# X and C in one set of loads, and XA loaded whole and copied into place by GpSimd

## The chip, the cores and the metric

The kernel runs on one core of a Trainium2 chip. The metric is the device time of one execution in microseconds; the time given for a kernel is the median of its runs. A profile shows one execution, with the time of every instruction on the five engines (TensorE, VectorE, ScalarE, GpSimd, SyncE) and of the DMA traffic.

## The reference

The kernel computes three layers, one after the other, over 3072 tokens (4 batches of 768) of 256 features:

```
# 1. a state-space layer, per batch and head (8 heads of 32), in chunks of 32 tokens
L = exp(cum_i - cum_j), causal;  M = (C B^T) * L
y[chunk] = M @ x + (C @ state) * exp(cum)
state = exp(sum log a) * state + sum_j decay_j * B_j x_j^T
# 2. a mixture of 8 experts, one per token
e = argmax(x @ w_gate);  out = gate * relu(x @ w1[e]) @ w2[e]
# 3. a dense layer
out = relu(x @ w_in)^2 @ w_out
```

The change is in the first layer. There `x` is needed in two layouts: by chunk and position for the state update (called Xt here), and by position for `M @ x` (called XA). `C` is needed in two as well (Cb for `C B^T`, CT for `C @ state`).

## The kernel before

The function `attention` does layer 1 and the gating of layer 2. The work is cut into 6 phases (two batches by 256 tokens each) of 4 tiles (128 tokens by 256 features), 24 tiles in all. One loop, `for i in range(-2, 24)` (L672), issues everything in an order written out by hand; each engine works its own instructions strictly in that order and waits on semaphores for the others. In step `i` of the loop:

- `st_S(i + 2)` (L416): TensorE multiplies B by Cb into `sc` (L425), VectorE multiplies by the decays Qm into M (L428). It has work for two of the four tiles of a phase.
- `st_D(i + 2)` (L431): TensorE multiplies the decayed B (Bt) by Xt into `dS` (L444); `st_R(i + 2)` (L451): VectorE runs the state forward with it (L461). Both have work in even steps only.
- `st_Y(i)` (L463): TensorE adds up `M @ XA` (L473) and `CT @ state` (L480); VectorE scales the sum into `row` (L485).
- `prep(ph)` (L387), on GpSimd, makes Qm (L401) and Bt (L395, from the loaded B) of phase `i // 4 + 2`, in step 4n+2: two Qm, two Bt, two Qm, two Bt.
- the gating of finished tiles: transposes, `logits`, `gateA`, `gateB` (which ends in a store of the rows to the DRAM tensor `xs`, L572, on SyncE's queue), `spotA` (VectorE and ScalarE, and one GpSimd multiply into `hi`, L594) and `spotB` (TensorE on `hi`, L602). `row` has three buffers, so the row of phase 3 waits for the store of phase 0.

In this text S(n), D(n), R(n), Y(n) are the work of these functions for tile n; a phase ph has tiles 4ph to 4ph+3.

All loads of this stage are issued by SyncE, in program order, and each tile has two or three buffers. A phase needs: B (`load_b`, one load of 512 KB), CT (`load_t`, two loads of 128 KB), XC (`load_c`, L288: for each of four column blocks `c`, the partitions c, c+4, c+8, ...; Xt and Cb stand side by side in one row, 4 KB each), and XA (`load_x`, L293). XA is block-diagonal: block `c` of the columns is filled in partitions 32c to 32c+31 and is zero elsewhere. The zeros are written once before the loop, and `load_x` brings only the filled part, as four loads of 128 KB (32 partitions of 4 KB).

The order of the loads in the loop, for phases after the second: in step 4n+3 `load_b`, the C half of XC (four loads of 128 KB, `load_c(nx, XS)`, L687), later in the same step XA of the phase before that one (four loads of 128 KB, L751), then CT; in the step after, the Xt half of XC (four loads of 128 KB, L701). Phase 2 has both halves of XC together, in step 0, as four loads of 256 KB. A load waits on SyncE until the last reader of its buffer is done: an XA load for Y of the phase two before it.

The host arranges XA in DRAM as `[phase, 128, 1024]`, partition 32c + j holding block c's rows, so that the four loads of a phase read one contiguous 512 KB.

Of the kernel before, what the change touches and what calls it, by code (L numbers as in the profile page):

```python
# [9 lines left out]
F32 = mybir.dt.float32  # L10
# [232 lines left out]
def attention(tc, k, ctx):  # L243

    nc = tc.nc
    v, s, g, pe, sp = nc.vector, nc.scalar, nc.gpsimd, nc.tensor, nc.sync
# [5 lines left out]
    big = body.enter_context(tc.tile_pool(name="abig", bufs=1))  # L252
# [20 lines left out]
    XA = [(big if p else stp).tile([128, 4, 1024], F32, tag=f"XA_{p}", name=f"XA_{p}") for p in range(2)]  # L273
# [2 lines left out]
    Xr = [x.rearrange("p c (b f) -> p c b f", b=2) for x in XA]  # L276
    BB = [bigs[p // 2].tile([128, 2, 2, 256], F32, name=f"BB_{p}") for p in range(3)]
    CT = [bigs[p // 2].tile([128, 2, 2, 256], F32, name=f"CT_{p}") for p in range(3)]
    Bt = [big.tile([128, 2, 2, 4, 4, NS], F32, name=f"Bt_{p}") for p in range(2)]
    dS = [ps_1.tile([128, 4, 128], F32, name=f"dS_{p}") for p in range(2)]  # L280
    small = k.psk.tile([128, 512], F32, name="small")

    def load_b(ph):
        sp.dma_start(out=BB[ph % 3], in_=k.bb[ph])

    XT, XS = slice(0, 1), slice(1, 2)

    def load_c(ph, at=slice(0, 2), cs=(0, 1, 2, 3)):  # L288
        for c in cs:
            sp.dma_start(out=XC[ph % 2][c:128:4, c].rearrange("p (h f) -> p h f", h=2)[:, at],  # L290
                         in_=k.xc[at, ph, c:128:4].rearrange("h p f -> p h f"))

    def load_x(ph, cs=(0, 1, 2, 3)):  # L293
        for c in cs:
            at = slice(32 * c, 32 * c + 32)
            sp.dma_start(out=XA[ph % 2][at, c], in_=k.xa[ph, at])

    def load_t(ph):
        for h in range(2):
            sp.dma_start(out=CT[ph % 3][64 * h:64 * h + 64, h], in_=k.ct[ph, 64 * h:64 * h + 64])  # L300

# [18 lines left out]
    def zero_t(f, p):  # L320
        for h in range(2):
            o = CT[p][64 * h:64 * h + 64, 1 - h].rearrange("p a f -> p (a f)")
            f(o, zt[64 * h:64 * h + 64])
# [18 lines left out]
    s.activation(la, aa, ACTF.Ln)  # L342
    blank_x(v.tensor_copy, 0, 1)
    load_x(0, (2, 3, 0, 1))
    zero_t(v.tensor_copy, 0)

# [116 lines left out]
    def st_Y(i):  # L463
        ph, r = divmod(i, 4)
        p = ph % 2
        t2, b2 = divmod(r, 2)
        b, t = tile_tokens(i)
        M = Ms[ph, b2]
        y = ps_y.tile([128, 2, 128], F32, tag="y", name="y")
        for hq in range(2):  # L470
            for c in range(4):
                c8 = t2 * 4 + c
                pe.matmul(y[32 * c:32 * c + 32, hq], M[:, hq, c8, :],  # L473
                          Xr[p][:, :, b2, c8 * 64 + hq * 32:c8 * 64 + hq * 32 + 32],
                          start=(hq == 0), stop=False, skip_group_check=True)
        st = states[b, t]
        for hq in range(2):
            for c in range(4):
                s0 = t2 * 128 + c * 32
                pe.matmul(y[32 * c:32 * c + 32, hq], CT[ph % 3][:, hq, b2, s0:s0 + 32], st[:, c],  # L480
                          start=False, stop=True, skip_group_check=True)
        if r == 0:
            rows[ph] = rowp.tile([128, 4, ROW], F32, tag="row", name="row")
        row = rows[ph][:, r]
        v.tensor_tensor(row[:, 0:DM].rearrange("p (h d) -> p h d", d=D), y.rearrange("p q (h d) -> p (q h) d", d=D),  # L485
                        Pd[:, b, t].unsqueeze(2).to_broadcast([128, 8, D]), ALU.mult)
# [30 lines left out]
    def logits2(ph):  # L517
        pe.transpose(small[:, 0:128], gts[ph], ident)
# [57 lines left out]
    def spotA(i, n, late=False):  # L576
        at = k.slots[:, i:i + n]
        lh = pl2.tile([128, 4], I32, tag="lh", name="lh")[:, 0:n]
        lf = pl2.tile([128, 4], F32, tag="lf", name="lf")
        v.tensor_scalar(lh, at, 7, None, ALU.logical_shift_right)  # L580
        v.scalar_tensor_tensor(lf[:, 0:n], lh, -128.0, at, ALU.mult, ALU.add)

        lo = pl2.tile([128, 4, 128], F32R, tag="lo", name="lo")
        hi = pl2.tile([128, 4, NE * NBL], F32R, tag="hi", name="hi")
        some = lambda c, m: cst[:, c:c + m].unsqueeze(1).to_broadcast([128, n, m])
        every = lambda x, m: x.unsqueeze(2).to_broadcast([128, n, m])
        if late:
            v.tensor_tensor(lo[:, 0:n], some(C_LO, 128), every(lf[:, 0:n], 128), ALU.is_equal)
        else:
            for r in range(n):  # L590
                s.activation(lo[:, r], cst[:, C_LO:C_LO + 128], ACTF.Abs, bias=lf[:, r:r + 1], scale=-1.0)
            s.activation(lo[:, 0:n], lo[:, 0:n].bitcast(F32), ACTF.Relu, bias=1.0, scale=-1.0)
        v.tensor_tensor(hi[:, 0:n], some(C_HI, NE * NBL), every(lh, NE * NBL), ALU.is_equal)
        (v if i == 20 else g).tensor_tensor(hi[:, 0:n], hi[:, 0:n].bitcast(F32), every(cst[:, C_ROW + i:C_ROW + i + n], NE * NBL),  # L594
                                         ALU.mult)
        spots[i] = lo, hi
# [37 lines left out]
    def stage(f, i):  # L634
        if 0 <= i < 24:
            f(i)
# [35 lines left out]
    for i in range(-2, 24):  # L672
        if i == 2:
            st_Y(2)
            st_TT(0)
            st_Y(3)
            zero_t(acopy, 2)
            load_t(2)
        if i == -2:
            st_R(0, (0, 1, 2, 3))  # L680
        stage(st_S, i + 2)
        if i >= 0 and i % 4 == 2 and i // 4 + 2 < NPH:
            prep(i // 4 + 2)
        nx = (i + 1) // 4 + 2
        if i % 4 == 3 and 2 < nx < NPH:
            load_b(nx)
            load_c(nx, XS)  # L687
        if i >= 0:
            stage(st_D, i + 2)
        if i % 2 == 0 and 2 < i < 22 and i not in (16, 20):  # L690
            st_TT(i - 2)
        if i in (8, 12):
            spotA(i - 8, 4)
        if i == 18:
            order()
        if i == 6:
            v.tensor_copy(Ub, cst[:, C_U:C_U + 128])
        if 0 <= i < 22:
            st_R(i + 2, (0, 1, 2, 3))
        if i >= 0 and i % 4 == 0 and i // 4 + 2 < NPH:  # L700
            load_c(i // 4 + 2, XT if i else slice(0, 2))  # L701
        if i == 0:
            sp.dma_start(out=cst[:, C_U:C_END], in_=k.consts[:, C_U:C_END])
        if i == 14:
            sp.dma_start(out=k.mc[0:T, :].rearrange("(p q) r -> p (q r)", p=128), in_=blank)
            sp.dma_start(out=k.xs[0:1, :], in_=pad[0:1])
        if i == 17:
            logits2(3)
            gateA(3, 12, 4)
            spotC(8)  # L710
        if i >= 0 and i not in (2, 3):
            st_Y(i)
        if i == 14:
            gateB(2, 8, 4)
            spotA(8, 4)
        if i in (16, 20):
            st_TT(i - 2)
        if i == 16:
            spotB(8, 4)
        if i == 21:  # L720
            logits(4)
        if i in (21, 23):
            st_T(i - 1)
        if i == 23:
            k.ring.low(0, v, 0, 2)
            st_L(20)
            st_L(21)
        if i in (9, 13):
            spotB(i - 9, 4)
        if i in (5, 9, 13, 21):  # L730
            logits2(i // 4 - 1)
            if i in (9, 13):
                spotC(i - 9)
            gateA(i // 4 - 1, i - 5, 4)
        if i == 17:
            gateB(3, 12, 4)
            spotA(12, 4)
        if i == 18:
            spotB(12, 4)
            spotC(12)  # L740
            pick(k.first, 0, 1, 0, 2)
        if 4 <= i <= 16 and i % 4 == 0:
            logits(i // 4 - 1)
        if i == 22:
            st_T(21)
            gateB(4, 16, 4)
            k.ring.high(0)
            k.ring.load(2)
            k.ring.load(3)
        if i >= 3 and i % 4 == 3 and i // 4 + 2 < NPH:  # L750
            load_x(i // 4 + 2)  # L751
        if i % 4 == 3 and 2 < nx < NPH:
            load_t(nx)
        if i in (7, 11):
            gateB(i // 4 - 1, i - 7, 4)
        if i == 18:
            k.moe = Moe(k, tc, k.c2, m0)
            k.ring.aim(0)
            k.moe.load_rows((0, 0))
        if i == 19:  # L760
            k.ring.stage(stp, "XA_0")
            for n in range(2):
                k.ring.load(n)
            early.close()
            k.ring.grow(k.ringpool(), 5)
# [813 lines left out]
```

## Time and profile before

| what | before |
|---|---|
| median of 3 runs (lowest to highest) | 511.66 us (511.46 to 514.49) |
| the profiled execution's own time | 510.4 us |
| its span on the core | 508.4 us |
| TensorE, VectorE, ScalarE, GpSimd busy | 491.3, 372.4, 309.4, 99.4 us |
| DMA traffic | 51.22 MB, mean 101 GB/s |
| granted TensorE clock | 0.998 of full speed |

The span runs from the first to the last instruction. An engine is busy while it executes; TensorE's instructions overlap in its pipeline and their ends are modelled. Layer 1 takes about the first 78 us; the other two layers are long rows of matmuls behind it. A row of a timeline gives the start in us, the time in us, the engine, the line of the kernel, the operation, output and inputs, and how many instructions are merged; in square brackets stands how long the engine had idled before, and which event the profile takes to have ended that. SPq is SyncE's queue of DMA issues: its time is that of the issuing, the data land some microseconds later.

### The profile page before, as it was taken

How to read it: one execution, taken by the hardware profiler on the slowest of the kernel's cores; microseconds unless marked ns; L12 is line 12 of the kernel's file. 1: busy time of each engine (PE TensorE's matmuls, PEld its weight loads, DVE VectorE, ACT ScalarE, POOL GpSimd, SP SyncE). 2: the span in 40 equal slices, each digit the busy share in tenths (PEclk: the TensorE clock that was granted, in tenths of full speed). 3: DMA queues.
4: the chain of work that ended last, by engine and by line, in shares of the span. 5: the costliest groups of instructions: out<-in, count | busy, mean ns of one | idle time of the engine just before them, and what ended most of it. 6: DMA issues, size and time to landing. Idle time of an engine off the chain costs nothing.

```text
span 508.4 us, 11650 instructions
## 1 busy us (share of the span) xinstructions
PE 491.3 (97%) x4537; PEld 459.1 (90%) x4537; DVE 372.4 (73%) x844; ACT 309.4 (61%) x636; POOL 99.4 (20%) x131
## 2 busy tenths in 40 slices
PE   7899798999999999999999999999999999999995
PEld 3677678899999999999999999899999999999995
DVE  8787688669898899994666767534888888676521
ACT  8332335376656666755986889776555555455684
POOL 6953210543331130000000000101500300031031
PEclk9999999999999999999999999999999999999999
DMA  8886866767676656530001100000100000010010
GB/s 258 271 254 219 276 196 209 227 163 191 188 222 169 176 193 191 183 84 2 2 1 43 43 0 1 12 10 12 74 2 0 23 23 1 1 43 1 1 43 24
DMA packets 20476, 51.22 MB, mean 101 GB/s; under 512 B 6561, under 2 KB 6690, under 8 KB 20418
## 3 DMA queue, kind: packets, MB, share of 16 engines
q1 hardware_dynamic: 17442, 43.04, 27.2%
q0 software_dynamic: 2832, 7.01, 5.1%
q8 instruction: 37, 0.61, 0.5%
q10 hardware_dynamic: 144, 0.40, 0.2%
q14 instruction: 21, 0.17, 0.1%
HBM read 44.06 MB, written 6.37 MB: 99 GB/s over the span
## 4 chain that ended last, share of the span: by engine, by line
PE 85%; issue 4%; ACT 3%; DVE 3%; DMA 2%; POOL 1%; SPq 1%; ACTq 0%; another core or an unknown queue 0%; POOLq 0%; DVEq 0%
PE u L1261 24%; PE o L953 14%; PE h L937 14%; PE h L1081 11%; PE h L1169 9%; PE u L1169 2%; DMA XC<-in_xc_dram 2%; PE dS L444 2%; PE y L473 2%; PE sc L425 2%; PE y L480 1%; PE tpm L918 1%; ACT XC L312 1%; PE tp L502 1%; DVE st L461 1%
## 5 line engine op out<-in xcount | busy, mean ns | idle before, releaser
L1261 PE MATMUL u<-wol,ga 128*128 128x256 f32 x384 | 108.0, 281 | 0.0
L1261 PE MATMUL u<-woh,ga 128*128 128x256 f32 x384 | 107.7, 281 | 0.0
L1261 PE MATMUL u<-woh,gb 128*128 128x256 f32 x384 | 107.7, 280 | 0.0
L1275 POOL DMA_INDIRECT out_dram<-ob,idx x24 | 26.6, 1109 | 278.9 <-ACT ob L1274 274.3
L1088 DVE TENSOR_TENSOR gb<-q,ga 128x256 fp32r<-128x256 f32 (+1 forms) x64 | 35.7, 558 | 57.5 <-ACT ga L1087 57.4
L1261 PEld LDWEIGHTS u<-woh,ga 128*128 128x128 f32 x384 | 72.3, 188 | 1.4
L1261 PEld LDWEIGHTS u<-wol,ga 128*128 128x128 f32 x384 | 72.3, 188 | 1.3
L1261 PEld LDWEIGHTS u<-woh,gb 128*128 128x128 f32 x384 | 72.5, 189 | 0.1
L940 ACT ACTIVATE hh<-h 128x256 fp32r<-128x256 f32 (+8 forms) x72 | 33.9, 472 | 52.6 <-PE h L937 49.0
L1081 PE MATMUL h<-zz,wih 128*128 128x512 f32 (+1 forms) x192 | 59.1, 356 | 0.0
L942 DVE SCALAR_TENSOR_TENSOR hl<-h,hh 128x256 fp32r<-128x256 f32 (+8 forms) x72 | 38.2, 530 | 16.9 <-ACT hh L940 16.8
L953 PE MATMUL o<-hl,whi 128*128 128x256 f32 (+8 forms) x144 | 47.6, 331 | 0.1
L953 PE MATMUL o<-hh,whi 128*128 128x256 f32 (+8 forms) x144 | 47.7, 331 | 0.0
L953 PE MATMUL o<-hh,wlo 128*128 128x256 f32 (+8 forms) x144 | 47.4, 329 | 0.2 <-DVE wlo L174 0.2
L937 PE MATMUL h<-xh,whi 128*128 128x208 f32 (+7 forms) x128 | 44.3, 346 | 0.2 <-DVE hl L942 0.2
L174 DVE TENSOR_TENSOR wlo<-wst,whi 128x512 fp32r<-128x512 f32 x64 | 43.2, 676 | 0.0
L937 PE MATMUL h<-xh,wlo 128*128 128x208 f32 (+7 forms) x128 | 42.9, 335 | 0.0
L937 PE MATMUL h<-xl,whi 128*128 128x208 f32 (+7 forms) x128 | 42.8, 335 | 0.0
L1085 ACT ACTIVATE q<-h 128x256 f32<-128x256 f32 (+1 forms) x64 | 30.9, 482 | 13.2 <-PE h L1081 11.3
L1081 PEld LDWEIGHTS h<-zz,wih 128*128 128x128 f32 x192 | 34.9, 188 | 4.3
L1169 PE MATMUL h<-zz,s 128*128 128x256 f32 x216 | 38.4, 286 | 0.0
L883 POOL DMA_INDIRECT xr<-xs,where x27 | 27.6, 1024 | 41.9 <-PE tpm L918 26.6
(250 smaller groups left out, 1191.6 us busy)
## 6 DMA issues: line engine op xcount, KB each, us to landing
wst<-in_wq_dram SPq DMA_DIRECT2D x32, 512.0 KB, 4.8
w<-in_win_dram SPq DMA_DIRECT2D x8, 512.0 KB, 6.5
w<-in_wout_dram SPq DMA_DIRECT2D x8, 512.0 KB, 4.3
XC<-in_xc_dram SPq DMA_DIRECT2D x28, 128.0 KB, 4.1
xs<-row SPq DMA_DIRECT2D x6, 516.0 KB, 4.0
BB<-in_bb_dram SPq DMA_DIRECT2D x6, 512.0 KB, 4.2
XA<-in_xa_dram SPq DMA_DIRECT2D x24, 128.0 KB, 3.8
XC<-in_xc_dram SPq DMA_DIRECT2D x10, 256.0 KB, 4.4
```

The lines of the kernel that those rows point to most:

```text
L174: eng.tensor_tensor(lo[:, w], st[:, w], hi[:, w].bitcast(F32), ALU.subtract)
L883: k.nc.gpsimd.indirect_dma_start(out=self.xr[key][:, j], out_offset=None, in_=rows, in_offset=bass.IndirectOffsetOnAxis(ap=at, axis=0))
L937: nc.tensor.matmul(ps, ring.up(wt, e, f, kd), xt[:, kd], start=(i == 0), stop=(i == 5))
L940: nc.scalar.activation(a, ps, ACTF.Relu)
L942: rest = lambda: nc.vector.scalar_tensor_tensor(b, ps, 0.0, a.bitcast(F32), ALU.max, ALU.subtract)
L953: nc.tensor.matmul(self.yps[e][d][:, c:c + n], ring.down(wt, e, f, d), ht, start=(f == 0 and i == 0), stop=(f == 7 and i == 2))
L1081: nc.tensor.matmul(ps, wt[:, kd, m * 128:m * 128 + 128], zt[t][:, kd], start=(i == 0), stop=(i == 5))
L1085: nc.scalar.activation(q, ps, ACTF.Relu)
L1088: nc.vector.tensor_tensor(b, q, a.bitcast(F32), ALU.subtract)
L1169: mm(o, w, z, start=start and i == 0, stop=True, skip_group_check=True)
L1261: nc.tensor.matmul(o, gt[:, q * 128:q * 128 + 128], wt[:, m], start=(m == first and i == 0 and h == 0), stop=(m == last and i == 2), skip_ ...
L1275: ins = nc.gpsimd.indirect_dma_start(out=k.out, out_offset=bass.IndirectOffsetOnAxis(ap=self.idx[:, c:c + 1], axis=0), in_=ob, in_offset=N ...
```

## The change

XC of phases 3 to 5 is loaded whole, in step 4n+4, by four loads of 256 KB; the separate C loads in step 4n+3 are gone. XA of phases 2 to 5 is loaded by one DMA of 512 KB into a new buffer `xin` (one buffer, 128 partitions of 4 KB), in the place where `load_x` stood, and a new function `place` has GpSimd copy the four blocks of 32 partitions to their columns of XA. For phase 2 and phase 5 the copies are issued right behind the load (steps 3 and 15), for phase 3 and 4 in steps 8 and 12, behind `spotA`. Phases 0 and 1 are loaded as before, and the bytes that are moved are the same.

```diff
+    xin = big.tile([128, 1024], F32, name="xin")
...
+    def place(ph):
+        for c in range(4):
+            at = slice(32 * c, 32 * c + 32)
+            g.tensor_copy(XA[ph % 2][at, c], xin[at])
...
         if i % 4 == 3 and 2 < nx < NPH:
             load_b(nx)
-            load_c(nx, XS)
         if i >= 0:
             stage(st_D, i + 2)
...
         if i in (8, 12):
             spotA(i - 8, 4)
+            place(i // 4 + 1)
...
         if i >= 0 and i % 4 == 0 and i // 4 + 2 < NPH:
-            load_c(i // 4 + 2, XT if i else slice(0, 2))
+            load_c(i // 4 + 2)
...
         if i >= 3 and i % 4 == 3 and i // 4 + 2 < NPH:
-            load_x(i // 4 + 2)
+            sp.dma_start(out=xin, in_=k.xa[i // 4 + 2])
+            if i in (3, 15):
+                place(i // 4 + 2)
```

## Rows read from the trace of the kernel before

**Rows 1.** The page, busy time of each engine: us, share of span, instructions.
```profile
PE 491.3 (97%) x4537; PEld 459.1 (90%) x4537; DVE 372.4 (73%) x844; ACT 309.4 (61%) x636; POOL 99.4 (20%) x131
```

**Rows 2.** Stretches: length; busy PE, PEld, DVE, ACT, POOL (instructions); clock, DMA share, GB/s.
```profile
20.00:78.00 58.00, 52.30 (x1295) 40.90 (x1287) 45.88 (x184) 18.60 (x54) 20.73 (x42) 1.00 0.74 234
20.00:32.00 12.00, 10.34 (x265) 7.87 (x261) 10.18 (x37) 2.52 (x7) 6.64 (x14) 1.00 0.93 289
...
42.00:52.00 10.00, 8.40 (x219) 6.45 (x212) 7.75 (x33) 3.17 (x11) 3.15 (x7) 1.00 0.67 204
52.00:64.00 12.00, 10.14 (x249) 7.85 (x246) 8.23 (x34) 4.01 (x12) 3.12 (x7) 1.00 0.87 281
```

**Rows 3.** Timeline of SyncE's DMA issues, 25 to 50 us.
```profile
25.79 3.03 SPq L290 DMA_DIRECT2D XC<-in_xc_dram  x4
28.86 3.79 SPq L296 DMA_DIRECT2D XA<-in_xa_dram  x4
...
45.44 0.52 SPq L572 DMA_DIRECT2D xs<-row  x1
46.05 3.81 SPq L290 DMA_DIRECT2D XC<-in_xc_dram  x4
```

**Rows 4.** Timeline of TensorE, 35 to 59 us.
```profile
35.80 0.64 PE L473 MATMUL y<-XA,M 128*32 128x128 f32 x16 [0.25 <-PE tp L502]
...
38.32 0.59 PE L602 MATMUL small<-hi,lo 128*128 128x32 f32 x4
...
39.02 1.07 PE L425 MATMUL sc<-XC,BB 128*32 128x256 f32 x16
...
51.89 1.08 PE L444 MATMUL dS<-XC,Bt 128*32 128x128 f32 x32 [1.22 <-DMA XC<-in_xc_dram]
...
58.71 0.64 PE L473 MATMUL y<-XA,M 128*32 128x128 f32 x16 [1.16 <-DVE st L461]
```

**Rows 5.** The chain of waits: start, us, what, just before 51.89 us.
```profile
47.97 3.83 DMA XC<-in_xc_dram
```

**Rows 6.** The last XA load of phase 4: issue times in ns, starts, landing in us.
```profile
L296 SPq DMA_DIRECT2D XA<-in_xa_dram x1: 422/422/422, 55.3 to 55.3; - x1
...
DMA to landing us min/median/max: 3.2/3.2/3.2
```

**Rows 7.** Timeline of VectorE, 45 to 56 us.
```profile
45.35 0.16 DVE L581 SCALAR_TENSOR_TENSOR lf<-lh,slots 128x4 f32<-128x4 int32 x1
...
49.65 0.76 DVE L485 TENSOR_TENSOR row<-y,Pd 128x256 f32<-128x256 f32 x2 [1.86 <-DMA xs<-row]
...
55.83 0.30 DVE L581 SCALAR_TENSOR_TENSOR lf<-lh,slots 128x4 f32<-128x4 int32 x1
```

**Rows 8.** The four C loads issued from 25.8 us: min/median/max ns, starts, landing.
```profile
L290 SPq DMA_DIRECT2D XC<-in_xc_dram x4: 488/595/1037, 25.8 to 27.8; - x4
...
DMA to landing us min/median/max: 6.3/6.6/6.7
```

**Rows 9.** The page, DMA issues: number, KB each, median us to landing.
```profile
BB<-in_bb_dram SPq DMA_DIRECT2D x6, 512.0 KB, 4.2
```

**Rows 10.** GpSimd by line and shape: number, busy us, mean ns, idle before.
```profile
L401 POOL TENSOR_TENSOR Qm<-cst,Q 128x256 f32<-128x256 f32 x24 | 14.4, 621 | 0.0
...
L665 POOL MEMSET Bt<- 128x1024 f32 x1 | 1.0, 952 | 0.0
```

**Rows 11.** Timeline of GpSimd, 0 to 36 us.
```profile
0.36 0.10 POOL L1567 MEMSET const-float32-0.0<- 128x1 f32 x1 [0.36 <-issue]
0.39 0.10 POOL L1567 MEMSET const-float32-1.0<- 128x1 f32 x1
...
26.41 1.20 POOL L401 TENSOR_TENSOR Qm<-cst,Q 128x256 f32<-128x256 f32 x2
32.01 0.76 POOL L395 TENSOR_TENSOR Bt<-BB,Fd 128x128 f32<-128x128 f32 x2 [4.39 <-PE y L480]
...
35.22 0.40 POOL L594 TENSOR_TENSOR hi<-hi,cst 128x128 fp32r<-128x128 f32 x1 [0.57 <-DVE hi L593]
```

## The prediction

> **What bounds it now.** Read the page's busy time first: TensorE is busy 97% of the span, so only TensorE's idle time can be won [rows 1]. The change touches the attention stage alone, whose loop runs to 78 us. The table by stretch shows the size of the prize: from 20 to 78 us TensorE is busy 52.30 of 58 us, so at most 5.7 us, 1.1% of the span, can be gained, and the idle lies thickest in 42 to 64 us (1.6 and 1.9 us) [rows 2]. The rest of the kernel sees the change only as a start that is earlier or later.
>
> Next SyncE's timeline, in order of time [rows 3]: four loads of one half of XC take 3.0 or 3.8 us to issue, four of XA 3.8 us. SyncE is late: the store of `xs` that step 7 asks for is issued at 45.44, the Xt loads of phase 4 that step 8 asks for at 46.05, when TensorE is at step 12. On TensorE's timeline the delay comes out at three places [rows 4]. Y(8) idles 0.25 us at 35.80, just behind the last XA load of phase 2. D(16) idles 1.22 us until 51.89; the chain of waits puts it down to the Xt load issued at 47.97, landed at 51.80 (47.97 + 3.83) [rows 5]. Y(16) idles 1.16 us until 58.71; the row blames VectorE, but Y(16) uses nothing of that instruction, and the last XA load of phase 4, issued at 55.3, took 3.2 us to land: 58.5 [rows 6]. VectorE also waits 1.86 us at 49.65 for the late store [rows 7], no longer than TensorE's own stall there.
>
> **The change, part by part.** I call a step's work S, D, R, Y as the code does; a load's landing counts from its issue.
>
> *Fewer issues.* C of phases 3 to 5: twelve issues go. XA of phases 2 to 5: sixteen become four. At 0.60 us for one of C and 0.42 for one of XA [rows 6, 8] that is 12 us of SyncE, 20 with the waits in the rows above. C now comes with Xt, a step later, behind `xin` and two CT loads. For phase 3: the DMA engines are full until 32 us; at the 289 GB/s of that stretch [rows 2] `xin`, CT and XC together (1.75 MB) need 6 us more, 38. S(12) wants them at 39.02 [rows 4]: hidden, with 1 us to spare. XC of phase 4 is out by 40 (below), ten microseconds ahead of D(16).
>
> So the stalls of D(16) and Y(16) go: 1.22 + 1.16 = 2.38 us. What is late next there is VectorE: R(16) needs spot, gate and M first, and without the 1.86 us wait these end about 1.3 us earlier than now, so little of the gain is held back. Lower bound of the gain 1.2 us (one of the two is replaced), upper 2.6 (with the 0.25 of Y(8)).
>
> *One load, then copies.* The `xin` load of phase 2 goes out at 25.79, where C's loads stand now. The same 512 KB in the same place, the four C loads issued from 25.8 to 27.8, took 6.3 us or more each, the last landing at 34.1 [rows 8]. A single 512 KB load (BB) took 4.2 us at the median [rows 9]: 30.0. But the DMA engines are full here (share 0.93 [rows 2]), so I take 34.1, the row in the same place, with 30.0 as the other end.
>
> The trace has no GpSimd copy. The nearest row of the size is a memset of 1024 columns, 0.95 us, which only writes. GpSimd's two-input work takes 0.40 us for 128 columns and 0.62 for 256 [rows 10, 11], so 1.72 ns a column; half of that for one input plus the 0.18 that is left gives 1.06 us. Ends: 0.95 and 0.18 + 1.76 = 1.94 us. I take 1.06.
>
> Four copies are 4.2 us if one waits for the other. They share no partition, however, each filling 32 of 128. All wide GpSimd instructions in the trace follow each other with 0.04 us of overlap; only the small memsets at the start, 0.10 us each, begin 0.03 us apart [rows 11], so an instruction can begin while the one ahead is still under way. Bounds for the four: 1.06 + 0.09 = 1.15 us and 4 x 1.06 = 4.2 (7.8 with the dear copy). I take 1.15, nearest to the row where the engine isn't filled. The Trainium skill says this outright (GPSIMD Engine Reference, Instruction dispatch): each of the eight cores owns 16 partitions and starts the next instruction as soon as it has finished its share, while others may still be writing. By that rule the four run beside each other; by the wide rows alone they would not. No row here shows copies of 32 partitions.
>
> *The wait it adds.* GpSimd's queue is in order. It now has, between prep(2) and prep(3), four copies that wait for `xin`. Before, GpSimd did the first two Qm of prep(3) at 26.41, the rest from 32.01 and `hi` of the first four tiles at 35.22 [rows 11]. Afterwards: copies from 34.1 to 35.3; Y(8) at 35.8 still finds its rows. Then prep(3): four Qm and four Bt, 2 x (1.20 + 0.76) = 3.9 us, to 39.2; then `hi`, 0.40 us, 39.6. Who waits: the matmuls of spotB(0), at 38.32 now [rows 4], which stand in TensorE's queue ahead of S(12). They start at about 39.75: 1.4 us late, on the path. Bt for D(12) is ready by 37.3, in time.
>
> The later places are covered: `xin` of phase 3 waits for these copies (35.3), lands 4.2 later at 39.5 and is copied behind `hi`, to 40.9. Y(12) is four steps behind Y(8), 11 us at the 2.9 us a step between Y(8) and Y(16) [rows 4]; prep(4) then ends near 45, well ahead of D(16). Queued behind that waiting load on SyncE are CT(4), the store of `xs` and XC(4): out by 40.2, against 46 to 50 before. Phases 4 and 5 have more room still. If that cover were gone each would cost what phase 2 costs.
>
> *Collisions.* A GpSimd instruction and a VectorE one can hold each other up: lf at 55.83 took 0.30 beside GpSimd's Bt, 0.16 at 45.35 [rows 7]. During the first copies VectorE does three such small operations for `hi`: 3 x 0.14 = 0.4 us, hidden, since `hi` waits for GpSimd anyway. I cost it at 0, at most 1 us (one copy).
>
> **Sum.** -2.38 + 1.43 = -0.95 us. The profiled execution took 510.4 us (span 508.4 and 2.0 around it), so 509.45; the median of the runs, 511.66, lies 1.26 above the profiled one, so 510.7 as a median.
>
> **Rivals.**
>
> *Slower: the copies run one after the other.* Place: GpSimd in phase 2. Copies 34.1 to 38.4 (Y(8) is late already), prep(3) to 42.3, `hi` to 42.7, spotB(0) at 42.8: 4.5 us late, less 2.38: +2.1, median 513.8. It decides from 2.1 us for the four copies upwards: there the loss passes the gain. For it: every wide pair of GpSimd instructions is serial. Against: none of those leaves partitions free. 0.30.
>
> *The same with dear copies* (1.94 us each): spotB(0) 8 us late, +5.6, 517.3. Against: a memset of the same columns took 0.95. 0.05.
>
> *No lateness:* `xin` lands by 32.6 since one load is issued faster than four. Then only the gain is left: -2.4 to -2.6, 509.2. For: a 512 KB load takes 4.2 us elsewhere. Against: the full DMA engines. 0.13.
>
> *The stalls change owner.* Once loads are early, R on VectorE or the collisions hold D and Y. VectorE is busy 46 of 58 us [rows 2]. Gain 1.2 instead of 2.4 and the 1.4 stays: +0.2, 511.9. The Trainium skill warns of this (Perfetto Trace Analysis, Optimizing Scalar/DVE Operations): GpSimd and VectorE share a read port, so moving work between them may not help. If each of three operations waited for a copy of 1.06, R(10) would be 3 us late, of which the lateness of `hi` hides about two. 0.07.
>
> *The change doesn't do what it says:* the same bytes through the same engines, so that landings stay as late. Phases 4 and 5 speak against it (share 0.67 in 42 to 52 us [rows 2]: engines idle while SyncE issues). It is inside the case above.
>
> **How the numbers follow.** Forecast 0.45 (510.7, its own range 509.2 to 511.9), then 0.30, 0.13, 0.07, 0.05. The range reaches from the case without lateness, with a bit for the 2.6 gain and the spread of runs, 508.6, over the serial case, 513.8, with 1 us for a copy somewhat dearer: 514.8. It leaves out the dear copies and what I haven't thought of. One per cent, 5.1 us, is about what a measurement of this kernel tells from no change. Faster by that would need nearly all idle time of the stage: 0.02. Slower by it needs the dear copies: 0.06. The same: 0.92.
>
> **What would show it.** The four copies of phase 2 in the trace: their starts 0.03 us apart or 1 us apart, their mean near 1.06, the first at about 34. spotB(0) waiting for `hi` of GpSimd near 39.7. D(16) and Y(16) without a wait for a load. SyncE idle between loads from 42 us on. The forecast falls if the copies are serial, if `xin` lands well before 33, or if D(16) and Y(16) get another wait as long.

## The result: slower, 514.51 us

The changed kernel takes 514.51 us (median of 21 runs, 513.22 to 516.75), the kernel before 510.95 beside it (21 runs); the ratio is 1.0082, 95% interval 1.0066 to 1.0097. The profiled execution has a span of 512.8 us against 508.4. A second measurement of the same kernel gave 1.0098 (1.0060 to 1.0135). The forecast was 510.7 us, a small gain.

**Stretches of the profile after** answer to [rows 2]: length; busy PE, PEld, DVE, ACT, POOL; granted clock, DMA share, GB/s.

```profile
20.00:78.00 58.00, 49.36 (x1209) 38.72 (x1205) 47.71 (x170) 16.01 (x46) 36.95 (x58) 0.97 0.70 226
...
32.00:42.00 10.00, 6.63 (x154) 5.26 (x142) 6.56 (x19) 2.67 (x7) 8.24 (x13) 0.85 0.69 232
42.00:52.00 10.00, 8.77 (x203) 6.75 (x207) 8.55 (x32) 1.58 (x6) 8.36 (x14) 0.98 0.98 312
...
64.00:78.00 14.00, 12.03 (x307) 9.59 (x310) 11.69 (x46) 3.82 (x12) 6.03 (x7) 1.00 0.31 113
```

The profile before has, from 32 to 42 and from 64 to 78 us:

```profile
32.00:42.00 10.00, 9.62 (x247) 7.66 (x243) 8.19 (x34) 3.30 (x10) 5.30 (x12) 1.00 0.70 216
...
64.00:78.00 14.00, 13.80 (x337) 11.07 (x335) 11.53 (x50) 5.60 (x15) 2.52 (x3) 1.00 0.55 181
```

GpSimd is busy 36.95 us of the 58, 20.73 before. TensorE loses busy time between 32 and 42 us (6.63, 9.62 before) and between 64 and 78 us (12.03, 13.80 before).

**SyncE and GpSimd after**, two timelines, answering to [rows 3] and [rows 11]. First SyncE's issues:

```profile
25.07 0.43 SPq L758 DMA_DIRECT2D xin<-in_xa_dram  x1
...
27.77 2.88 SPq L292 DMA_DIRECT2D XC<-in_xc_dram  x4
...
40.17 3.13 SPq L292 DMA_DIRECT2D XC<-in_xc_dram  x4
```

```profile
33.53 4.31 POOL L303 COPY XA<-xin 32x1024 f32<-32x1024 f32 x4 [6.75 <-PE small L568]
37.93 1.20 POOL L408 TENSOR_TENSOR Qm<-cst,Q 128x256 f32<-128x256 f32 x2
...
41.68 0.40 POOL L601 TENSOR_TENSOR hi<-hi,cst 128x128 fp32r<-128x128 f32 x1
```

XC of phase 4 goes out at 40.17 (46.05 before), as forecast. The xin load of phase 2, issued at 25.07, lands at 33.41 us (the row of the copies names TensorE's L568, which ended at 33.06), and then four copies take 4.31 us where 1.15 was forecast. The whole of prep(3) stands behind them, and `hi` behind that. All sixteen copies, from the group of their line:

```profile
L303 POOL COPY XA<-xin x16: 1026/1033/1079, 33.5 to 66.7; 32x1024 f32<-32x1024 f32 x16
```

**TensorE after**, timeline, answering to [rows 4]:

```profile
37.90 0.65 PE L480 MATMUL y<-XA,M 128*32 128x128 f32 x16 [2.38 <-POOL XA L303]
...
42.14 0.69 PE L609 MATMUL small<-hi,lo 128*128 128x32 f32 x4 [0.65 <-POOL hi L601]
...
42.94 1.07 PE L432 MATMUL sc<-XC,BB 128*32 128x256 f32 x16
...
50.33 0.49 PE L451 MATMUL dS<-XC,Bt 128*32 128x128 f32 x9 [1.09 <-issue]
...
55.76 1.06 PE L451 MATMUL dS<-XC,Bt 128*32 128x128 f32 x32
...
61.22 0.62 PE L480 MATMUL y<-XA,M 128*32 128x128 f32 x16
...
68.00 0.18 PE L564 MATMUL small<-erb,ones 128*128 128x32 bf16 x1 [1.43 <-DVE spot L614]
...
68.22 1.07 PE L432 MATMUL sc<-XC,BB 128*32 128x256 f32 x16
```

Y(8) waits 2.38 us for the copies, spotB(0) then waits for `hi` and starts at 42.14 instead of 38.32. D(16) at 55.76 and Y(16) at 61.22 wait for no load any more. Two new stalls stand further down: 1.09 us inside the row of D(14), put down to "issue", and 1.43 us at 68.00 on VectorE (0.33 at that place before).

**VectorE after**, timeline, answering to [rows 7]:

```profile
33.68 0.91 DVE L587 TENSOR_SCALAR lh<-slots 128x4 int32<-128x4 int32 x1
34.62 1.03 DVE L588 SCALAR_TENSOR_TENSOR lf<-lh,slots 128x4 f32<-128x4 int32 x1
...
66.04 0.66 DVE L550 SCALAR_TENSOR_TENSOR oh<-sh,cst 128x32 f32<-128x32 f32 x1
66.96 0.82 DVE L556 TENSOR_TENSOR hot<-oh,m 128x32 bf16<-128x32 f32 x1
```

Small operations of the gating that took 0.16 to 0.19 us take 0.53 to 1.03 us while a copy runs (the 0.53 is `oh` at 43.66).

**The account.** Starts of the same TensorE work, after minus before, in us; the second trace is that of the repeated run g1_after_again:

| | forecast | first trace | second trace |
|---|---|---|---|
| S(12), before at 39.02 | +1.43 | +3.92 | +4.70 |
| S(12) to S(16) | 0 | +1.35 | +1.20 |
| S(16) to D(16) | -1.22 | -1.40 | -1.40 |
| D(16) to Y(16) | -1.16 | -1.36 | -1.36 |
| Y(16) to S(20), before at 64.06 | 0 | +1.66 | +1.19 |
| sum | -0.95 | +4.17 | +4.33 |

Behind that little changes in these two traces: the spans are 4.4 and 4.5 us longer. The +1.35 is the "issue" stall. The +1.20 is clock: TensorE had waited 2.48 us for the copies, and then worked at the lower of its levels (1.2 instead of 2.4 GHz) for a part of the next stretch, as the granted clock of the second trace shows:

```profile
42.00:52.00 10.00, 9.56 (x183) 7.09 (x185) 7.40 (x29) 1.02 (x4) 8.57 (x15) 0.79 0.80 272
```

### The profile page after: what moved, and what is told of

Same layout as the page of the kernel before. It is cut to its first block, busy times and chain, and to the rows that moved or that the text cites. A ratio compares the mean times of both kernels' runs of the same rounds, so it can differ in the third digit from the quotient of the medians.

```text
span 512.8 us, 11629 instructions
## 1 busy us (share of the span) xinstructions
PE 492.2 (96%) x4537; PEld 459.8 (90%) x4537; DVE 377.3 (74%) x844; ACT 309.7 (60%) x636; POOL 116.8 (23%) x147
## 4 chain that ended last, share of the span: by engine, by line
PE 82%; DVE 5%; issue 4%; ACT 3%; POOL 2%; DMA 2%; ACTq 0%; POOLq 0%; another core or an unknown queue 0%; DVEq 0%
PE u L1270 24%; PE h L946 13%; PE o L962 13%; PE h L1090 11%; PE h L1178 9%; PE u L1178 2%; DVE st L468 2%; PE dS L451 1%; PE sc L432 1%; PE tpm L927 1%; PE y L480 1%; PE y L487 1%; PE tp L509 1%; DMA xr<-xs,where 1%; POOL out_dram L1284 1%
## 5 line engine op out<-in xcount | busy, mean ns | idle before, releaser
L946 PE MATMUL h<-xl,whi 128*128 128x208 f32 (+7 forms) x128 | 42.8, 335 | 0.0
L892 POOL DMA_INDIRECT xr<-xs,where x27 | 28.7, 1061 | 35.5 <-PE tpm L927 20.3
```

The costliest lines, as they stand in the source:

```text
L892: k.nc.gpsimd.indirect_dma_start(out=self.xr[key][:, j], out_offset=None, in_=rows, in_offset=bass.IndirectOffsetOnAxis(ap=at, axis=0))
L946: nc.tensor.matmul(ps, ring.up(wt, e, f, kd), xt[:, kd], start=(i == 0), stop=(i == 5))
```

## The experiments

Every ratio is to runs of the kernel before on the same chip, with its 95% interval.

### The halves apart

Loads alone (e1, repeated as h4): the change without xin and copies.

```diff
-            sp.dma_start(out=xin, in_=k.xa[i // 4 + 2])
-            if i in (3, 15):
-                place(i // 4 + 2)
+            load_x(i // 4 + 2)
```

> The changed kernel without its second half: XC whole in four loads of 256 KB, XA by four loads as before, no copies. Theory 1 (four copies in a row are late in phase 2, +3.8 us, and VectorE's small operations collide with copies, +3.2 us; the loads alone gain 2.8): the gain alone, 2 to 3 us faster than before, ratio 0.994 to 0.996; no wait for a load at D(16) and Y(16). Theory 2 (only the lateness in phase 2 costs, collisions are hidden): the same. Theory 3 (a step later, C is late and the merged loads cost): as slow as before or slower, S(12) or S(16) waits for XC.

> The kernel of e1_xc_whole once more (XA as before, XC of phases 3 to 5 whole), for a second measurement beside the others. Theory 1 (S(12) waits 1.2 us for XC of phase 3 and the clock drops behind it, the gain at D(16) and Y(16) is 2.7): ratio 0.998 (0.995 to 1.001), a little worse than h3_c3_early_again. Theory 2 (merged loads are a gain whole): 0.992 to 0.996.

Measured 0.9947 (0.9916 to 0.9979) and, repeated, 1.0021 (0.9996 to 1.0045). D(16) and Y(16) wait for no load in either trace. In the first, though not in the second, S(12) waits for XC of phase 3, which I had called hidden:

```profile
40.51 1.07 PE L432 MATMUL sc<-XC,BB 128*32 128x256 f32 x16 [1.20 <-DMA XC<-in_xc_dram]
```

Keeping C of phase 3 early (f1, repeated as h3) removes that wait:

```diff
             load_b(nx)
+            if nx == 3:
+                load_c(nx, XS)
...
-            load_c(i // 4 + 2)
+            load_c(i // 4 + 2, XT if i == 4 else slice(0, 2))
```

> XA as before; XC of phases 4 and 5 whole, C of phase 3 early and apart as before. Theory 1 (twelve fewer issues free SyncE; the wait of S(12) seen in e1_xc_whole is the price of bringing C of phase 3 a step later): S(12) without a load wait, D(16) and Y(16) still without; the 1.2 us of S(12) come on top of e1's gain: ratio to before 0.992 (0.989 to 0.996). Theory 2 (SyncE is late in phase 3 again with the split loads, so D(16) or Y(16) waits again): 0.995 to 0.999.

> The kernel of f1_c3_early once more (XA as before, C of phase 3 early and apart, XC of phases 4 and 5 whole), for a second measurement. Theory 1 (merged loads of phases 4 and 5 remove the waits of D(16) and Y(16), 2.4 to 2.8 us): ratio 0.996 (0.993 to 0.998). Theory 2 (what they gain is lost to late instruction fetches of TensorE, as in f1's profile): 0.998 to 1.002.

Measured 1.0006 (0.9973 to 1.0038) and 1.0012 (0.9984 to 1.0039). The gain that I expected was missed both times. Of four measurements of the loads' half only the first is clear of 1.000, and its repetition doesn't bear it out: two waits, 2.38 us together, are gone from the traces, and no gain in the time is shown.

The other half alone (g2): XA by xin and copies, C and Xt apart as before.

```diff
             load_b(nx)
+            load_c(nx, XS)
...
-            load_c(i // 4 + 2)
+            load_c(i // 4 + 2, XT if i else slice(0, 2))
```

> One part alone: XA by xin and copies as in the changed kernel, C and Xt in separate loads as before. Theory 1 (copies cost, merged loads gain): spotB(0) late by 3.5 to 5 us, D(16) or Y(16) keep a part of their waits for a load, ratio 1.009 to 1.014, worse than the changed kernel. Theory 2 (the late C of the merged loads is what costs): ratio 1.000 to 1.004, better than the changed kernel.

Measured 1.0176 (1.0143 to 1.0210): the copies' half brings the whole loss, and more. In its trace SyncE issues xin later (at 29.07, landing at 35.09), and the copies of phase 4 now make `hi` of a later spotB late as well:

```profile
39.62 1.08 PE L480 MATMUL y<-XA,M 128*32 128x128 f32 x16 [2.71 <-POOL XA L303]
...
68.19 0.62 PE L609 MATMUL small<-hi,lo 128*128 128x32 f32 x4 [2.57 <-POOL hi L601]
```

The changed kernel as it is, with the kernel before once more beside it:

> The changed kernel, unchanged, once more. Theory 1 (the loss is the four serial copies of phase 2, then VectorE's collisions): copies 1.04 to 1.09 us apart, spotB(0) late by 3.5 to 4 us against the kernel before, ratio 1.008 (1.005 to 1.011). Theory 2 (the loss of the first profile is partly an instruction fetch of TensorE that came late by chance in the row of dS at 50.33 us): that stall of 1.09 us is gone or elsewhere, and the ratio is 1.004 to 1.008.

> The kernel before, unchanged, once more, for a profile on the chip of the experiments. Theory 1 (the half-clock stretches between 82 and 111 us in the profiles of the experiments, and times near 516 us, belong to this chip and stage): the same drop of the clock here in 80 to 110 us, ratio 1.000 (0.997 to 1.003). Theory 2 (they come from the edits): full clock there, as in the first profile of before.

Measured 1.0098 and, for the kernel before, 1.0021 (0.9998 to 1.0044), so that 0.2% lie between two measurements of one kernel. The loss of phase 2 repeats (the account above). The 1.09 us stall of D(14) doesn't; the lower clock is in its place. The question about 80 to 110 us is settled by repetitions: all eight traces of e1 to e4 and f1 to f4 lose 3.3 to 4.3 us between 95 and 100 us, behind layer 1, against the first trace of before, and no trace of g, h or k does, though h4 is the kernel of e1 and h3 that of f1. So that loss belongs to no edit, and the kernel before took longer too beside those runs (516.5 and 516.3 us, 509.6 to 511.0 beside the others).

### Are copies on disjoint partitions serial?

The kernel before with copies (e3) or memsets (e4) of a scratch buffer, 32 partitions by 1024 columns, that wait for nothing:

```diff
+    def extra(n):
+        for c in range(n):
+            at = slice(32 * (c % 4), 32 * (c % 4) + 32)
+            g.tensor_copy(sc0[at], sc0[at])      # e4: g.memset(sc0[at], 0.0)
...
             spotA(i - 8, 4)
+            extra(i // 4 + 3)
...
             load_x(i // 4 + 2)
+            if i in (3, 15):
+                extra(4 + i // 5)
```

> The kernel before with GpSimd copies added that touch nothing of the work: a scratch tile of 1024 columns, 32 partitions each, copied onto itself, four copies in step 3, five in step 8, six in step 12, seven in step 15, so that each batch reaches over VectorE's gating of the tiles before. The loads are as before and no copy waits for one. Theory 1: the gating's two operations with two SBUF inputs take 0.5 to 0.8 us instead of 0.19, and the kernel gets 1.5 to 3 us slower (ratio 1.003 to 1.006). Theory 2: no change (below 0.5 us). On whether copies of different partitions overlap: if they do, four take little over 1 us from first start to last end, if not 4.2.

> As the kernel with added copies, with memsets of the same 32 x 1024 columns in place of the copies: GpSimd as busy, but it only writes. If what collides is GpSimd's reading of SBUF with VectorE's second SBUF input, the gating's operations keep their 0.19 us and the time stays within 0.5 us of before. If what collides is any GpSimd work, this is as slow as with copies.

Measured 1.0044 (1.0008 to 1.0080) and 1.0003 (0.9968 to 1.0038). GpSimd's timeline and then the group of `hot` on VectorE between 20 and 78 us (minimum, median and maximum in ns), first of e3, then of e4:

```profile
27.10 4.26 POOL L304 COPY sc<-sc 32x1024 f32<-32x1024 f32 x4
```

```profile
L557 DVE TENSOR_TENSOR hot<-oh,m x4: 760/826/1430, 29.5 to 64.4; 128x32 bf16<-128x32 f32 x4
```

```profile
26.96 3.89 POOL L304 MEMSET sc<- 32x1024 f32 x4
```

```profile
L557 DVE TENSOR_TENSOR hot<-oh,m x5: 191/191/684, 29.0 to 77.4; 128x32 bf16<-128x32 f32 x5
```

Four independent instructions on four separate sets of partitions take four times one of them, copies and memsets alike. It is not the program's own waits that line them up: the third and the fourth of these copies wait for no semaphore, and start 1.07 and 1.08 us behind the one ahead. And `hot` takes 0.83 us at the median beside copies, 0.19 beside memsets of nearly the same length: what holds `hot` up goes with copies, which read SBUF, not with any GpSimd instruction. (The 0.68 in e4 stands beside a Qm, which reads SBUF too; but `oh` took 0.49 once beside a memset, and why stays open. 1.34 us in e3's trace are an "issue" stall, so its ratio is not the collisions' price alone.)

### What the length of the copies is worth

Copies of 64 columns instead of 1024, which leave most of XA stale: in all phases (f2), in phase 2 alone (f3), in phases 3 to 5 alone (h2).

```diff
     def place(ph):
+        n = 64                 # f3: 64 if ph == 2 else 1024; h2: 1024 if ph == 2 else 64
...
-            g.tensor_copy(XA[ph % 2][at, c], xin[at])
+            g.tensor_copy(XA[ph % 2][at, c, 0:n], xin[at, 0:n])
```

> The changed kernel with copies of 64 columns in place of 1024 (most of XA is left stale): every load, wait and order is the same, only the copies' work is gone. Theory 1 (the length of the serial copies is the whole loss): spotB(0) late by less than 1.5 us against before, lh, lf, oh, hot back near 0.2 us, ratio 0.994 (0.990 to 0.998). Theory 2 (the loss is the wait for xin in GpSimd's queue and the late XC, not the copies' work): ratio 1.002 to 1.008, spotB(0) late by 3 us or more.

> The changed kernel with copies of 64 columns in phase 2 alone (the rest of that XA is left stale); phases 3 to 5 copy whole. Theory 1 (3.8 us of the loss are phase 2's, 3.1 the collisions of phases 3 to 5): xin of phase 3 is issued near 34.5 us and its copies fit behind hi without delaying prep(4); about 0.2 us between loss and gain, ratio 1.000 (0.997 to 1.003). Theory 2 (as e2_phase2_direct showed, any full set of copies on GpSimd ahead of a prep is late, so the loss moves to phase 3): ratio 1.004 to 1.009, a TensorE wait of 1 us or more on GpSimd between 45 and 56 us.

> The changed kernel with copies of 64 columns in phases 3 to 5 (most of those XA are left stale); phase 2 copies whole. Theory 1 (of the loss, 3.8 to 4.1 us and the half-clock stretch behind it belong to phase 2, and 1.3 to 1.8 us between 59 and 68 us to copies that hold VectorE's oh, hot, lh, lf up): spotB(0) late by 3.5 to 4.2 us as before, hot of L556 at 0.2 us behind 60 us, no wait of 1.4 us on VectorE near 68; ratio 1.006 (1.002 to 1.009), 1 to 2 us better than the changed kernel. Theory 2 (the wait near 68 us has another cause): it stays, ratio 1.008 to 1.012.

Measured: f2 1.0055 (1.0024 to 1.0086), f3 1.0041 (1.0006 to 1.0076), h2 1.0078 (1.0048 to 1.0108). In f3's trace the lateness of phase 2 is gone: Y(8) and spotB(0) stand within 0.7 us of [rows 4], and wait for ScalarE at most.

```profile
36.11 0.64 PE L481 MATMUL y<-XA,M 128*32 128x128 f32 x16
...
38.95 0.59 PE L610 MATMUL small<-hi,lo 128*128 128x32 f32 x4 [0.45 <-ACT ls L522]
```

So the 3.8 us in the traces are the copies' length. In the time they are 0.4 to 0.6% (f3 against the two measurements of the changed kernel), with intervals that overlap. That f3 is slower than before all the same, theory 1 doesn't explain: at S(20) its trace is level with before (63.79 against 64.06 us), and behind a wait of 1.33 us for VectorE just ahead of that the granted clock is 0.57 from 64 to 68 us. In h2 spotB(0) is late by 3.08 us, and the stall near 68 us is gone (0.33 us, as in the kernel before; 1.63 in g1_after_again):

```profile
64.10 0.19 DVE L557 TENSOR_TENSOR hot<-oh,m 128x32 bf16<-128x32 f32 x1
...
64.50 0.18 PE L565 MATMUL small<-erb,ones 128*128 128x32 bf16 x1 [0.33 <-DVE spot L615]
```

That stall is the copies' collision with VectorE, as theory 1 had it; in the time it shows by 0.002 at most. But f2 misses: with the copies' work gone it should have been faster than the kernel before, and is 0.5% slower. Its trace has the gain at D(16) and Y(16), and a stall of another kind ahead of it. At S(20) the two cancel, and the execution is 0.17 us behind before; 3.3 us more come from there to 85 us, at the end of layer 1 and behind it:

```profile
36.92 0.41 PE L451 MATMUL dS<-XC,Bt 128*32 128x128 f32 x3 [2.38 <-issue]
...
64.23 1.07 PE L432 MATMUL sc<-XC,BB 128*32 128x256 f32 x16
```

### Other places for the copies

Phase 2 by `load_x` (e2); all copies on ScalarE (f4: `acopy` in place of `g.tensor_copy`); the xin load of phase 2 in step 0 (h1):

```diff
             load_c(i // 4 + 2)
+        if i == 0:
+            sp.dma_start(out=xin, in_=k.xa[2])
...
-            sp.dma_start(out=xin, in_=k.xa[i // 4 + 2])
+            if i > 3:
+                sp.dma_start(out=xin, in_=k.xa[i // 4 + 2])
```

> The changed kernel, but XA of phase 2 comes by the four loads as before; phases 3 to 5 by one load and copies. Theory 1: the 3.8 us of lateness go, collisions stay: within 1 us of before (ratio 0.998 to 1.002), spotB(0) near 38.3 us, VectorE's L549 and L543 (their lines there) still 0.5 to 0.8 us in place of 0.19. Theory 2: only gains are left, 2 to 3 us faster than before. Theory 3: slower than before.

> The changed kernel with the copies on ScalarE in place of GpSimd. Theory 1 (the loss is GpSimd's queue ahead of prep(3) and its collisions with VectorE): Qm, Bt and hi are on time, lh, lf, oh, hot near 0.2 us, ratio 0.995 (0.991 to 1.000). Theory 2 (four copies of 1 us in any engine's in-order queue, behind a wait for xin until 33.4 us, hold up what stands behind them; on ScalarE the transposes' copies and exponentials): ratio 1.002 to 1.010, TensorE waits on ScalarE of 1 us or more near 38 us.

> The changed kernel with the xin load of phase 2 moved from step 3 to step 0, right behind XC of phase 2. Theory 1 (the four copies of phase 2 cost because they start only when xin lands at 33.5 us and prep(3) and hi stand behind them): xin lands by 30 us, copies end by 34.5, hi by 39, spotB(0) late by less than 1.2 us, no drop of the clock near 40 us; ratio to before 0.999 (0.996 to 1.003), by 0.007 to 0.013 better than the changed kernel (1.0098 in g1_after_again). Theory 2 (the copies' place in time doesn't matter, they cost by holding VectorE up or by their work on GpSimd): ratio 1.005 to 1.010.

e2 measured 1.0084 (1.0054 to 1.0113), a miss: the loss moved to phase 3, whose xin, issued at 37.03, lands at 45.28, so that Y(12) waits for the copies as Y(8) had done:

```profile
49.80 0.64 PE L480 MATMUL y<-XA,M 128*32 128x128 f32 x16 [2.38 <-POOL XA L303]
...
54.03 1.04 PE L609 MATMUL small<-hi,lo 128*128 128x32 f32 x4 [0.88 <-POOL hi L601]
```

The cover that I had counted on for phase 3 (Y(12) 11 us behind Y(8)) fails here by the landing: this xin takes 8.25 us. In the changed kernel, where TensorE is late already, it is issued at 37.87 and takes 3.63.

f4 measured 1.0618 (1.0573 to 1.0662). ScalarE's copies take 4.3 us too, and its queue waits 12.13 us for xin of phase 2; TensorE waits for what stands behind, four times:

```profile
37.74 0.86 PE L518 MATMUL small<-xt,cst 128*32 128x128 f32 x10 [11.19 <-ACT xt L512]
...
55.04 1.01 PE L609 MATMUL small<-hi,lo 128*128 128x32 f32 x4 [4.75 <-ACT ls L521]
```

The granted clock is 0.56 between 32 and 42 us there. A copy behind a late load costs most in the queue that TensorE needs most often.

h1 measured 1.0057 (1.0032 to 1.0081), 0.4% below the repeated changed kernel (the two intervals overlap), though short of what I expected. GpSimd's timeline, then TensorE's:

```profile
31.70 4.30 POOL L303 COPY XA<-xin 32x1024 f32<-32x1024 f32 x4 [4.86 <-DMA xin<-in_xa_dram]
...
39.97 0.40 POOL L601 TENSOR_TENSOR hi<-hi,cst 128x128 fp32r<-128x128 f32 x1
```

```profile
37.06 0.41 PE L451 MATMUL dS<-XC,Bt 128*32 128x128 f32 x3 [1.23 <-issue]
...
40.84 0.59 PE L609 MATMUL small<-hi,lo 128*128 128x32 f32 x4 [0.45 <-ACT ls L521]
```

GpSimd is off TensorE's path: spotB(0) waits for ScalarE, as it does in kernels without copies. What is left of the lateness are stalls put down to "issue", 0.98, 1.23 and 0.92 us, and the one on VectorE near 66 us (1.61).

### Where the loads' gain goes

Two ideas. The first: the waits of D(16) and Y(16) are slack, so that whatever is late earlier is late in their place. The traces with the loads of before speak for it: the two waits come to 2.38, 1.46 (g0), 1.73 (e3) and 0.39 us (e4, which was 2.1 us late before them). To test it, S(13) is issued four times over, 2.6 us of TensorE, in the kernel before (k1) and with C of phase 3 early (k2):

```diff
-        for hq in range(2):
+        for hq in (0, 1) * (4 if i == 13 else 1):
```

> The kernel before, with the eight matmul calls of S(13) issued four times over (the same values again), which makes TensorE 2.6 us later near 43 us. Theory 1 (the load waits of D(16) and Y(16) are slack: work that is late earlier is late in their place): the waits at D(16) and Y(16) fall below 0.5 us together, at TensorE's row for Y(16) no more than 1.2 us of the 2.6 are left, ratio to before 1.001 (0.998 to 1.004). Theory 2 (they are a loss of their own, whatever comes earlier): both waits stay near 1.2 us, Y(16) 2.6 us late, ratio 1.005 (1.002 to 1.008).

> The same four-fold S(13) in the kernel of f1_c3_early and h3_c3_early_again, where D(16) and Y(16) wait for no load. Theory 1 (no slack is left there): all 2.6 us are still there behind Y(16), ratio to before 1.006 (1.003 to 1.009), which is 0.005 over the two runs without the addition. Theory 2 (something else takes lateness up as well): ratio 1.000 to 1.003.

Measured 1.0068 (1.0043 to 1.0092) and 1.0056 (1.0033 to 1.0080). k1's trace does what theory 1 says: before D(16) it is 4.41 us behind the first trace of before (1.8 of them from ahead of S(12), where two "issue" stalls stand), behind Y(16) 1.62, and both rows start without a wait:

```profile
54.90 1.06 PE L444 MATMUL dS<-XC,Bt 128*32 128x128 f32 x32
...
60.35 0.62 PE L473 MATMUL y<-XA,M 128*32 128x128 f32 x16
```

The times say the opposite: 3.5 us slower, as theory 2 had it. So slack is seen in single executions and not borne out by the median; as an explanation it fails this test. The trace is no sure witness of the time either: it is 1.54 us behind at 80 us and 5.6 at its end, 3.2 of them from between 350 and 400 us, in work that the edit doesn't touch. k2 came out as its theory 1 had it, 0.0047 over the two runs without the addition.

The second: TensorE's instructions come late. The trace's DMA packets include packets of instructions; the one next to the stall of D(14) in the changed kernel, in 47.90 to 49.00 us:

```profile
q8 instruction: 1, 0.02, 5.7%
```

It ends at 48.93, and TensorE goes on at 50.33. Of all stalls of 0.3 us or more that are put down to "issue" between 24 and 62 us, 19 in nineteen traces (f4's left out), each ends 1.2 to 1.6 us behind the end of such a 16 KB packet, though such packets come only about every 6 us. And 16 of the 19 stand at three places of the program: ahead of the last 8, 3 or 9 matmuls of D(8), D(10) or D(14). These stalls come to 0 to 1.9 us, 0.7 on average, in seven traces with C and Xt apart, and to 0 to 3.1 us, 1.2 on average, in twelve with XC whole in some phase. The spread is as large as the difference. One place is clearer: in all seven traces with xin in phase 2 and copies on GpSimd, f2's among them, the row of D(10) takes 1.68 to 3.86 us, with a pause ahead of its last 3 matmuls; in the other thirteen it takes 1.08 to 1.58. The DMA engines are busy 0.93 to 1.02 of the time between 32 and 36 us in those seven, and 0.47 to 0.75 in ten of the thirteen. Whether their load makes the packet late is not shown; this is a lead and no proof. More traffic alone didn't bring them: 512 KB more in five steps, from ScalarE's queue,

```diff
+        if i in (3, 5, 7, 9, 11):
+            s.dma_start(out=sc0, in_=k.xa[i // 2 % 6])
```

> The kernel before with 512 KB more in each of the steps 3, 5, 7, 9 and 11, issued by ScalarE into a scratch buffer that nobody reads. Theory 1 (TensorE's instructions are fetched by the same DMA engines and come late behind packed data): a stall of TensorE of 0.5 us or more inside a row of dS that ends 1.3 to 1.7 us behind the end of a 16 KB instruction packet, and ratio 1.003 to 1.010 with longer load waits at D(16) or Y(16). Theory 2 (instruction packets pass the data): no stall put down to issue over 0.4 us between 28 and 60 us, ratio 0.999 to 1.004.

measured 1.0304 (1.0262 to 1.0346), most of it in waits for loads (5.47 us for XC at 34.32, 2.65 and 3.46 for XA at 46.02 and 61.31), with one stall of 0.45 us on "issue". Theory 1 missed there, and theory 2 on the time; that a TensorE that waits for data gives its instructions time to arrive is a guess.

## Why the prediction was wrong

**The step that failed** is the length of the four copies ("I take 1.15, nearest to the row where the engine isn't filled"): they take 4.31 us. The rows spoke against me: every wide pair of GpSimd instructions in [rows 11] is serial. I set that aside for the small memsets that start 0.03 us apart, and because the copies share no partition. The rule of the Trainium skill that I leaned on (GPSIMD Engine Reference, Instruction dispatch), that a core goes on to the next instruction while others still work, did not bring the overlap that I drew from it: 1.07 us from start to start for copies of 1.03 us, in e3 without anything to wait for. Whether a core without partitions in a copy is held for its length all the same, no run shows. My remark that "by the wide rows alone they would not" run beside each other leads to the rival's number.

**The rival "the copies run one after the other"**, 0.30, is what happened: copies to 37.84 (38.4 there), `hi` at 41.68 (42.3), spotB(0) at 42.14 (42.8). Its total, +2.1 us, is too small by 2.1, for two terms that I had at nothing. The stated range holds 514.51 only because it was stretched over this rival; the forecast of a gain fell. In the medians the copies' length is a third to somewhat over a half of the 0.8 to 1.0% (f2 has 1.0055 without it in all phases, f3 1.0041 without it in phase 2); the rest has no shown cause.

**Collisions**, "cost it at 0, at most 1 us", are 1.2 to 1.7 us in the traces, and not at the first copies, where `hi` waits anyway, but between 59 and 68 us, which the sum left out: `oh` and `hot` stand there on the way to TensorE's next row. I had cited the Trainium skill (Perfetto Trace Analysis, Optimizing Scalar/DVE Operations) on the read port that GpSimd and VectorE share; e3 and e4 agree with it (0.83 us beside copies, 0.19 beside memsets). A rule that I quoted as a rival should have been followed to each of the four places.

**What a wait brings with it** was not in the sum at all: behind the wait of phase 2 came 1.20 us of lower clock in one trace of the kernel and a stall of 1.35 us put down to "issue" in the other. That the wait brought on the second is not shown.

**The gain** was sized right against that trace (2.38 forecast, 2.76 measured in both traces), and is not shown as a gain in the time: the loads' half alone is 0.9947 to 1.0021. A wait that is read off one execution was 0.39 to 2.38 us in four. XC of phase 3 at 38 us, "hidden, with 1 us to spare", came at 36.84 in the changed kernel, but S(12) waited 1.2 us for it in e1 and e2.

**Right** were the landing of xin (34.1 forecast, 33.41 measured), one copy (1.06 and 1.03 us), the release of SyncE (XC of phase 4 by 40.2), and, in both traces of the changed kernel, that the end of the stage is all that reaches the rest.

**Open**: what takes the gain of the merged loads, and why f2, without the copies' work, is still 0.5% slower; the pause in D(10) that comes with xin is the nearest lead. No version here beats the kernel before beyond doubt: the one that did (e1) did not when repeated.

## What to carry to other kernels

Trading DMA issues for copies on another engine is priced by that engine's queue: the copies' full length, one after the other, counts from the landing of the load, and everything issued behind them is late by it. Look for the nearest row of the same size before trusting that work on separate partitions overlaps. Size a stall from several executions, since the wait of one may be half of it in the next.

## What the runs showed of the hardware

GpSimd worked off 32-partition instructions on disjoint partitions one at a time: 4.26 us for four copies, 3.89 for four memsets, and ScalarE was no faster (4.29). Beside copies, VectorE's `hot`, with two inputs in SBUF, took 0.83 us at the median instead of 0.19, beside memsets of that size 0.19; other small operations took between 0.16 and 1.03 us beside copies. And TensorE stood still for up to 2.38 us in the middle of a row of independent matmuls, with its data there, until 1.2 to 1.6 us behind the end of a packet of instructions.
